# Five-tile second-layer loop begun tile by tile, and two row transposes issued by ScalarE

## The chip, the cores and the metric

One NeuronCore of one Trainium2 chip runs the whole program. The metric is device time in microseconds (us) of one execution; the time shown for a kernel is the median of its runs. PE is TensorE (PEld its weight loads), DVE is VectorE, ACT is ScalarE, POOL is GpSimd, SP is SyncE, whose queue (SPq) issues nearly all DMAs.

## The reference

Three stages follow each other. Causal attention with a cumulative bias (2 batches, 8 heads, 576 positions, 64 wide) gives a matrix x of 1152 tokens by 512. A dense layer follows, and then a routed layer with 8 experts:

```python
h = x @ w_in                      # 512 -> 2048
g = h * np.cos(h)
x = g @ w_out                     # 2048 -> 512

logits = x @ w_gate               # 8 experts
expert_idx = np.argmax(logits, axis=1)
...                               # softmax weight; each expert takes up to 288 tokens, in order
h = np.maximum(np.einsum('ecd,edf->ecf', disp, w1), 0.0)    # 512 -> 1024
y = np.einsum('ecf,efd->ecd', h, w2)                        # 1024 -> 512
out[i] = gate_w[i] * y[expert_idx[i], pos[i]]
```

## The kernel before, in words

Matrix products are made from pairs of float16 numbers (a high and a low part), three products each. After attention, `l1` (L509) makes g for 16 blocks f of 128 hidden columns and 3 chunks of 384 tokens: 48 groups of 12 matmuls, each in a PSUM bank that ACT and DVE read (L522, L523, L531) before it is free again. Six banks (tags s, pt and mm, two each) rotate; two more have the tags xv and sm.

The second matmul of the dense layer works on nine token tiles of 128 tokens, T0 to T8. `l2_mm` (L566) issues the three matmuls of one tile and one f into the tile's bank, 48 matmuls for a tile. `l2_wide` (L572) takes the first five tiles at once: T0 in bank xv, T1 in bank sm, T2 to T4 in the next banks of the rotation, which the last groups of `l1` have just used. Its loop goes over f outside and over the tiles inside, so that the sequence of PE is f = 0 of T0 to T4, then f = 1 of T0 to T4, and so on. At each f it first calls `feed` twice; that is the decoding of one more block of w_out (L456 to L458, then the split at L428 on ACT and L429 on DVE) and, when these are through, the loads (L672, L676) and splits of the first expert's eight weight pieces. `wout_dec` puts the decoding of block f behind the last eviction of block f + 8 of `l1`.

When a tile's 48 matmuls are done, `l2_end` (L555) writes its row buffer: ACT the high part (L561), DVE the low part (L562), POOL the token number (L563).

Then comes routing. `route_a` (L594) brings the row into transposed form: for T0 to T6 with one DMA transpose from the row buffer into a tile `xr` (two buffers) issued on SP's queue (L598), for T7 and T8 with PE transposes (L603, with ACT copies at L559 and L605). `route_b` (L608) makes the logits on PE (L620, 12 small matmuls), then a chain of small steps on DVE (L630 to L649), ACT (L631, L640) and PE (L637 to L639), and last an indirect DMA on POOL's queue (L650) that scatters the rows to their experts' places in a DRAM buffer `disp`.

`l2r` (L812) interleaves this with the second matmul of T5 to T8: T0 is transposed at step 0, T1 at step 2, and so on; a step is two f, or six matmuls, and routing's second half follows two steps later. T5 comes at step 10, T6 at step 16. After T4 and after T7, `partial` (L860) picks the expert that has the most tokens so far; SP reads its number into a register (L873), and only then can the weights of that expert be loaded. Before T7's second half, `hook` (L1013) gathers the first two experts' rows from `disp` by DMA transposes on SP's queue (L716, L723), which needs the scatters of T0 to T6 to have landed. Expert weights pass through three staging buffers `ws` of 512 KB; a load waits until ACT (L428) and DVE (L429) have split the piece that lay there.

The order in which each engine and each queue executes is fixed when the program is built. A planner goes through the program by its own estimate of when each instruction is ready, with program order as the priority, so a later instruction may be placed before an earlier one. At run time each engine and queue waits in that fixed order. The planner also adds all waits, on data and on buffers.

Of the kernel before, what the change touches and what calls it, by code (L numbers as in the profile page):

```python
# [11 lines left out]
F16 = mybir.dt.float16  # L12
# [11 lines left out]
WO0 = 8  # L24
W3P = 12
L2F = 2
NK = 3
NF = 1
NH = 2
PT = 5  # L30
WN = 5
# [40 lines left out]
def kernel(ctx, tc, q, k, v, s, w_in, w_out, wg, w1, w2, out, cap, wide):  # L72
    nc = tc.nc
    B, H, S, D = q.shape
    NP = H // 2
    DM, DFF = w_in.shape
    E, _, F = w1.shape
# [3 lines left out]
    KF = DFF // 128  # L81
# [10 lines left out]
    PTILE = PT - 1  # L92
    R0 = E - NK
    PROFILES = [[min(n, NS) for n in p] for p in SIZES]
    LIMITS = [[(n + 1) * E for n in p[NK:]] + [BIG * -1.0] * NH + [n + 1 for n in p[:NK]] for p in PROFILES]

# [22 lines left out]
    def bank(tag, bufs=2, dt=F32):  # L119
        return ps.tile([128, 512], dt, tag=tag, bufs=bufs, name=f"ps_{tag}")  # L120

    def any_bank():
        t, b = BANKS[rot[0] % 3]
        rot[0] += 1
        return bank(t, b)
# [429 lines left out]
    def l2_end(T, xp):  # L555
        r = work.tile([128, ROW], I32, tag="row", name="row", bufs=6)
        xf = xq[:, 0:DM] if T >= NDT else None
        if T >= NDT:
            nc.scalar.activation(xf, xp, AF.Copy, scale=2.0 ** -2)  # L559
        rh = r[:, 0:DM].bitcast(F16)  # L560
        nc.scalar.activation(rh[:, 0:DM], xp, AF.Copy, scale=2.0 ** -8)  # L561
        nc.vector.scalar_tensor_tensor(rh[:, DM:2 * DM], xp, 2.0 ** -8, rh[:, 0:DM], ALU.mult, ALU.subtract)  # L562
        nc.gpsimd.tensor_copy(r[:, DM + 1:ROW], tokid[:, T:T + 1])  # L563
        rows[T] = (r, xf)

    def l2_mm(xp, T, f):  # L566
        c, i = divmod(T, TPC)
        ts = slice(i * 128, (i + 1) * 128)
        for n, (a, w_) in enumerate(((0, 0), (0, 1), (1, 0))):
            gate["pe"] = nc.tensor.matmul(xp, lhsT=G[c][:, a, f, ts], rhs=wout[w_][:, f, :], start=(f == 0 and n == 0), stop=(f == KF - 1 and n == 2))  # L570

    def l2_wide(tiles, feed, per):  # L572
        xps = {T: bank(*WT[i]) if i < len(WT) else any_bank() for i, T in enumerate(tiles)}
        for f in range(KF):
            for _ in range(per):
                next(feed, None)
            for T in tiles:
                l2_mm(xps[T], T, f)
            yield
        for T in tiles:  # L580
            l2_end(T, xps[T])
        yield
# [11 lines left out]
    def route_a(T):  # L594
        r, xf = rows[T]
        if T < NDT:
            xr = work.tile([128, 2 * KD, 128], F16, tag="xr", name="xr", bufs=2)
            nc.sync.dma_start_transpose(out=xr, in_=r[:, 0:DM].bitcast(F16))  # L598
            rows[T] = (r, xr)
        else:  # L600
            tp = bank("pt")
            for kk in range(KD):
                nc.tensor.transpose(tp[:, kk * 128:(kk + 1) * 128], xf[:, kk * 128:(kk + 1) * 128], idf)  # L603
            xt = xq[:, DM:2 * DM].rearrange("p (k t) -> p k t", k=KD)
            nc.scalar.copy(xt.rearrange("p k t -> p (k t)"), tp)  # L605
            rows[T] = (r, xt)
# [55 lines left out]
    def e_weights(plan, lo=0, hi=None):  # L662
        n = KD + KE // 2
        items = [(e, src, i) for e, src in plan for i in range(n)][lo:hi]
        pend = []

        def ld(e, src, i):
            t = staging()
            src = src() if callable(src) else src
            if i < KD:  # L670
                s1 = w1[e, i * 128:(i + 1) * 128, :] if src is None else w1v[bass.ds(src * DM + i * 128, 128), :]
                nc.sync.dma_start(t, s1)  # L672
            else:
                j = (i - KD) * 256
                s2 = w2[e, j:j + 256, :] if src is None else w2v[bass.ds(src * F + j, 256), :]
                nc.sync.dma_start(t.rearrange("p (a d) -> p a d", a=2), s2.rearrange("(a p) d -> p a d", p=128))  # L676
            pend.append(t)

        todo = list(items)

        def fill(n):
            while todo and len(pend) < n and not (callable(todo[0][1]) and todo[0][1]() is None):
                ld(*todo.pop(0))

        fill(len(ws) - 1)
        yield
        for e, src, i in items:
            fill(len(ws))
            b_ = (win, wb[0:2], wb[2:4], wout)[e % 4]
            a = [b_[0].rearrange("p a b -> p (a b)").rearrange("p (k c f) -> p k c f", k=KD, c=2), b_[1].rearrange("p a b -> p (a b)").rearrange("p (k c f) -> p k c f", k=KE, c=2)]  # L690
            ew[e] = a
            t = pend.pop(0)
            if i < KD:
                after("ev cnt", split, a[0][:, i, 0, :], a[0][:, i, 1, :], t, 64.0)
            else:
                j = (i - KD) * 2
                after("ev cnt", split, a[1][:, j:j + 2, 0, :], a[1][:, j:j + 2, 1, :], t.rearrange("p (a d) -> p a d", a=2), 64.0)
            yield
# [93 lines left out]
    def run(*gens):  # L792
        live = [[g, n, 0.0] for g, n in gens]
        while live:
            live.sort(key=lambda z: z[2])
            z = live[0]
            try:
                next(z[0])
                z[2] += 1.0 / z[1]
            except StopIteration:  # L800
                live.remove(z)

    def take(gen, n):
        for _ in range(n):
            next(gen, None)
            yield

    def seq(*gens):
        for g in gens:
            yield from g  # L810

    def l2r(tiles, hook):  # L812
# [13 lines left out]
        for T in tiles:  # L826
            for j in range(KF // 2):
                next(gen)
                if mid and step - mid[0][1] >= RD:
                    finish()  # L830
                if pend and step % RP == 0:
                    mid.append((pend[0], step))
                    route_a(pend.pop(0))
                step += 1
                yield
            pend.append(T)
        for T in pend:
            while mid and len(mid) >= 1:
                finish()
            mid.append((T, step))  # L840
            route_a(T)
# [7 lines left out]
    def fixed():  # L849
        V = nc.vector  # L850
        pick = P["pick"] = work.tile([1, NK, E], F32, name="pick", bufs=1)
        keys = P["keys"] = work.tile([1, E], F32, name="keys", bufs=1)
# [27 lines left out]
    def counts():  # L880
# [8 lines left out]
        fl = work.tile([1, 1], I32, tag="fl", name="fl", bufs=1)  # L889
        pr = work.tile([1, NK + NH, E], F32, tag="pr", name="pr", bufs=1)  # L890
        ov = work.tile([1, len(LIMITS), E + NH], F32, tag="ov", name="ov", bufs=1)
# [4 lines left out]
        for i in range(NH):  # L896
            V.tensor_tensor(pr[:, i, :], pp[0:1, E:2 * E], pick[:, i, :], ALU.mult)
        for i in range(NK):
            V.tensor_tensor(pr[:, NH + i, :], pp[0:1, 0:E], pick[:, i, :], ALU.mult)
# [12 lines left out]
    def registers(fl, si):  # L912
        order = [nc.values_load(si[0:1, r:r + 1], engines=SP, min_val=0, max_val=E - 1) for r in range(E - NK)]
        first = [nc.values_load(si[0:1, E + h:E + h + 1], engines=SP, min_val=0, max_val=(E - 1) * NS + HEAD) for h in range(NH)]
        return order, first
# [84 lines left out]
    with ExitStack():  # L1000
        if True:
# [4 lines left out]
            items = KD + KE // 2  # L1006
            pre = e_weights([(i, i if i < NF else (lambda i=i: P["o"][i] if i < len(P["o"]) else None)) for i in range(NK)])
            run((l2_wide(range(WN), seq(wo, take(pre, items + 1)), L2F), KF + 1))
            xa = early.enter_context(tc.tile_pool(name="xa", bufs=1, side="right"))
            e_buffers(xa)  # L1010
# [78 lines left out]
```

## Time and profile before

| | us |
|---|---|
| median of 3 runs | 465.89 (465.44 to 466.89) |
| the profiled execution's own time | 467.52 |
| span of its instructions | 465.6 |
| PE busy | 422.9 (91%) |
| DVE busy | 329.9 (71%) |
| ACT busy | 290.3 (62%) |
| POOL busy | 122.3 (26%) |

The profile is of one execution. Times in the trace are us from the first instruction. A line of the timeline gives the start, the length, engine, source line, operation, the tiles written and read, the shape and how many neighbours are merged in it; in square brackets stands how long the engine was idle before it and what ended that. Matmuls are pipelined: a merged row of three lasts longer than the step from it to the next row. The chain of waits follows the work that ended last back from the end. `SPq` rows show when SP issues a DMA, not when it lands.

### The profile page before, as it was taken

How to read it: one execution, taken by the hardware profiler on the slowest of the kernel's cores; microseconds unless marked ns; L12 is line 12 of the kernel's file. 1: busy time of each engine (PE TensorE's matmuls, PEld its weight loads, DVE VectorE, ACT ScalarE, POOL GpSimd, SP SyncE). 2: the span in 40 equal slices, each digit the busy share in tenths (PEclk: the TensorE clock that was granted, in tenths of full speed). 3: DMA queues.
4: the chain of work that ended last, by engine and by line, in shares of the span. 5: the costliest groups of instructions: out<-in, count | busy, mean ns of one | idle time of the engine just before them, and what ended most of it. 6: DMA issues, size and time to landing. Idle time of an engine off the chain costs nothing.

```text
span 465.6 us, 10963 instructions
## 1 busy us (share of the span) xinstructions
PE 422.9 (91%) x4036; PEld 289.4 (62%) x4036; DVE 329.9 (71%) x847; ACT 290.3 (62%) x674; POOL 122.3 (26%) x205
## 2 busy tenths in 40 slices
PE   1879998889999999999899999979799999988994
PEld 1556665666756665555344445434698899888962
DVE  7757889787899955788888665475571477667670
ACT  3867888787777776777722453253663576677670
POOL 7231323240125544545430002201002110220231
PEclk9989999999999999999999999999999999998998
DMA  5899998998995410121245755794869978977851
GB/s 122 228 182 183 176 177 178 191 195 222 282 293 199 137 48 0 45 77 67 86 154 174 232 147 125 176 283 119 261 188 223 139 204 290 294 267 276 284 175 45
DMA packets 112653, 83.14 MB, mean 179 GB/s; under 512 B 85430, under 2 KB 93622, under 8 KB 112591
## 3 DMA queue, kind: packets, MB, share of 16 engines
q1 hardware_dynamic: 110335, 77.63, 63.7%
q0 software_dynamic: 2256, 4.73, 3.1%
q8 instruction: 33, 0.54, 0.5%
q14 instruction: 29, 0.24, 0.2%
HBM read 57.47 MB, written 12.14 MB: 150 GB/s over the span
## 4 chain that ended last, share of the span: by engine, by line
PE 51%; DVE 15%; DMA 15%; issue 6%; ACT 6%; SPq 4%; POOL 2%; POOLq 0%; DVEq 0%; ACTq 0%
DMA ws<-in_moe_w_dram 10%; PE ps_mm L375 5%; PE ps_mm L570 4%; PE ps_s L517 4%; PE ps_pt L347 4%; PE ps_pt L517 3%; PE ps_mm L517 3%; PE ps_s L769 3%; PE ps_s L305 3%; DVE y L523 2%; PE ps_mm L747 2%; PE ps_pt L747 2%; PE ps_s L570 2%; PE ps_xv L570 2%; PE ps_pt L570 2%
## 5 line engine op out<-in xcount | busy, mean ns | idle before, releaser
L517 PEld LDWEIGHTS <-win 128*128 128x128 f16 x576 | 56.0, 98 | 40.3 <-issue 4.6
L570 PEld LDWEIGHTS <-gall 128*128 128x128 f16 x432 | 40.8, 98 | 49.3 <-issue 2.5
L570 PE MATMUL ps_mm<-wout,gall 128*128 128x512 f16 x240 | 56.3, 379 | 1.6 <-DVE n__3030 L531 1.6
L429 DVE SCALAR_TENSOR_TENSOR gall<-ws,gall 128x1024 f16<-128x1024 f32 x32 | 38.6, 1221 | 23.4 <-ACT gall L428 23.1
L428 ACT ACTIVATE gall<-ws 128x1024 f16<-128x1024 f32 x32 | 33.6, 1057 | 25.9 <-DMA ws<-in_moe_w_dram 25.7
L756 POOL DMA_INDIRECT out_dram<-gall,eM x16 | 20.5, 1282 | 100.6 <-ACT gall L755 92.9
L428 ACT ACTIVATE wout<-ws 128x512 f16<-128x512 f32 (+1 forms) x32 | 27.2, 860 | 26.5 <-DVE ws L458 18.3
L429 DVE SCALAR_TENSOR_TENSOR win<-ws,win 128x512 f16<-128x512 f32 (+1 forms) x32 | 31.2, 981 | 11.1 <-ACT win L428 10.2
L429 DVE SCALAR_TENSOR_TENSOR wout<-ws,wout 128x512 f16<-128x512 f32 (+1 forms) x32 | 30.4, 957 | 11.0 <-ACT wout L428 10.2
L308 ACT ACTIVATE z<-z,st 128x128 f32<-128x128 f32 (+3 forms) x64 | 35.4, 556 | 4.0 <-DVE st L307 3.6
L650 POOL DMA_INDIRECT disp<-row,rsli x9 | 9.8, 1089 | 92.9 <-ACT rm L631 48.5
L305 PE MATMUL ps_s<-kT,qT 128*128 128x128 f16 (+3 forms) x128 | 25.7, 310 | 9.3 <-DVE st L307 6.5
L517 PE MATMUL ps_s<-xT,win 128*128 128x384 f16 x192 | 34.1, 326 | 0.0
L517 PE MATMUL ps_pt<-xT,win 128*128 128x384 f16 x192 | 33.9, 326 | 0.0
L517 PE MATMUL ps_mm<-xT,win 128*128 128x384 f16 x192 | 33.8, 326 | 0.0
L428 ACT ACTIVATE win<-ws 128x512 f16<-128x512 f32 (+1 forms) x32 | 27.4, 860 | 9.8 <-DMA ws<-in_moe_w_dram 9.7
L375 PE MATMUL ps_mm<-pp,vf 128*64 128x128 f32 x320 | 33.0, 285 | 0.0
L307 DVE CUSTOM_DVE_ANT_0 z<-ps_s,zm 128x128 f32<-128x128 f32 (+3 forms) x64 | 29.2, 482 | 4.0 <-PE ps_s L305 3.9
L347 PE MATMUL ps_pt<-idf,z 128*128 128x128 f32 x160 | 29.5, 287 | 0.8 <-DVE pp L349 0.6
L747 PEld LDWEIGHTS <-gall 128*128 128x128 f16 x480 | 28.1, 97 | 1.8 <-DVE gall L429 0.8
L530 ACT ACTIVATE y<-y,quarter 128x384 f32<-128x384 f32 x48 | 29.1, 605 | 0.0
L375 PEld LDWEIGHTS ps_mm<-pp,vf 128*64 128x64 f32 x320 | 20.9, 136 | 9.2 <-issue 7.1
(523 smaller groups left out, 926.5 us busy)
## 6 DMA issues: line engine op xcount, KB each, us to landing
ws<-in_moe_w_dram SPq DMA_DIRECT2D x64, 512.0 KB
ws<-in_moe_w_in_dram SPq DMA_DIRECT2D x16, 512.0 KB
ws<-in_moe_w_out_dram SPq DMA_DIRECT2D x16, 512.0 KB
disp<-zc SPq DMA_DIRECT2D x18, 257.0 KB
out_dram<-zc SPq DMA_DIRECT2D x9, 256.0 KB
qf<-in_q_dram SPq DMA_DIRECT2D x16, 128.0 KB
kf<-in_k_dram SPq DMA_DIRECT2D x16, 128.0 KB
vf<-in_v_dram SPq DMA_DIRECT2D x16, 128.0 KB
```

The costliest lines, as they stand in the source:

```text
L305: nc.tensor.matmul(sp[:, 0:w], lhsT=qT[:, c, h * FULL + t, :], rhs=kk, start=(c == 0), stop=(c == 1))
L307: gate["dve"] = nc.vector.tensor_tensor_reduce(z[:, 0:w], sp[:, 0:w], zm[:, W512 + 128 - w:W512 + 128], SC, 3e38, ALU.add, ALU.min, st[:, ...
L308: nc.scalar.activation(z[:, 0:w], z[:, 0:w], AF.Exp, bias=st[:, 0, h:h + 1], scale=-1.0, accum_out=sm_[:, 0, h:h + 1])
L347: nc.tensor.transpose(pt[:, j * 128:(j + 1) * 128], zs[h][:, j * 128:(j + 1) * 128], idf)
L375: nc.tensor.matmul(xv[h * 64:h * 64 + 64, ts], lhsT=vf[:, h * FULL + j, :], rhs=pv[h][:, j * 128:(j + 1) * 128], start=(j == 0), stop=(j = ...
L428: nc.scalar.activation(hi, src, AF.Copy, scale=sc)
L429: (eng or nc.vector).scalar_tensor_tensor(lo, src, sc, hi, ALU.mult, ALU.subtract)
L517: nc.tensor.matmul(hp[:, 0:CH], lhsT=win[a][:, kk, fs], rhs=xT[:, x_, kk, xs], start=(n == 0), stop=(n == 3 * KD - 1))
L530: nc.scalar.activation(y, y, AF.Sin, scale=TWO_PI, bias=quarter)
L570: gate["pe"] = nc.tensor.matmul(xp, lhsT=G[c][:, a, f, ts], rhs=wout[w_][:, f, :], start=(f == 0 and n == 0), stop=(f == KF - 1 and n == 2))
L747: gate["pe"] = nc.tensor.matmul(hp[:, 0:ns], lhsT=a1[:, kk, a, fs], rhs=X[:, x_ * KD + kk, 0:ns], start=(n == 0), stop=(n == 3 * KD - 1))
L756: sc = nc.gpsimd.indirect_dma_start(out=out, out_offset=bass.IndirectOffsetOnAxis(ap=M[:, b, 1:2].bitcast(U32), axis=0), in_=y, in_offset= ...
```

## The change

There are two edits. `l2_wide` first calls `feed` for three f, then issues f = 0, 1, 2 for T0, then f = 0, 1, 2 for T1, and so on to T4; from f = 3 on the loop is as before. The number of matmuls, their operands and the banks are unchanged. And the DMA transposes of T5 and T6 (`T >= WN`, with WN = 5) are issued by ACT on its own DMA queue; those of T0 to T4 stay on SP's.

```diff
+FH = 3
...
     def l2_wide(tiles, feed, per):
         xps = {T: bank(*WT[i]) if i < len(WT) else any_bank() for i, T in enumerate(tiles)}
-        for f in range(KF):
+        for f in range(FH):
+            for _ in range(per):
+                next(feed, None)
+        for T in tiles:
+            for f in range(FH):
+                l2_mm(xps[T], T, f)
+        for f in range(FH, KF):
             for _ in range(per):
                 next(feed, None)
             for T in tiles:
...
             xr = work.tile([128, 2 * KD, 128], F16, tag="xr", name="xr", bufs=2)
-            nc.sync.dma_start_transpose(out=xr, in_=r[:, 0:DM].bitcast(F16))
+            (nc.scalar if T >= WN else nc.sync).dma_start_transpose(out=xr, in_=r[:, 0:DM].bitcast(F16))
```

## Rows read from the trace of the kernel before

**Rows 1.** Page, parts 0 and 1: the span and the busiest engine.
```profile
span 465.6 us, 10963 instructions
PE 422.9 (91%) x4036; PEld 289.4 (62%) x4036; DVE 329.9 (71%) x847; ACT 290.3 (62%) x674; POOL 122.3 (26%) x205
```

**Rows 2.** Busy time by stretch: window, length, PE, PEld, DVE, ACT, POOL, PEclk, DMA.
```profile
276.50:300.00 23.50, 22.97 (x188) 11.40 (x186) 14.72 (x85) 6.69 (x23) 5.31 (x7) 1.00 0.62 132
300.00:320.00 20.00, 17.12 (x98) 8.22 (x95) 12.54 (x23) 10.84 (x15) 3.12 (x4) 1.00 0.81 240
```

**Rows 3.** Timeline where the five-tile loop begins, PE and DVE.
```profile
223.37 0.81 PE L570 MATMUL ps_xv<-wout,gall 128*128 128x512 f16 x3
...
225.00 0.56 DVE L531 SCALAR_TENSOR_TENSOR n__3009<-ps_pt,y 128x384 f32<-128x384 f32 x1
...
227.43 0.56 DVE L531 SCALAR_TENSOR_TENSOR n__3030<-ps_mm,y 128x384 f32<-128x384 f32 x1 [0.35 <-POOL gall L539]
...
228.04 0.81 PE L570 MATMUL ps_mm<-wout,gall 128*128 128x512 f16 x3 [1.63 <-DVE n__3030 L531]
...
228.69 0.81 PE L570 MATMUL ps_xv<-wout,gall 128*128 128x512 f16 x3
```

**Rows 4.** Timeline where the five-tile loop ends and routing begins.
```profile
274.59 1.22 DVE L429 SCALAR_TENSOR_TENSOR win<-ws,win 128x1024 f16<-128x1024 f32 x1 [0.82 <-ACT win L428]
...
275.74 0.68 DVE L562 SCALAR_TENSOR_TENSOR row<-ps_xv,row 128x512 f16<-128x512 f32 x1
...
276.45 15.31 SPq L598 DMA_TRANSPOSE xr<-row  x6
...
281.14 0.45 PE L620 MATMUL ps_s<-wgs,xr 128*128 128x8 f16 x12
```

**Rows 5.** DMA view of 270 to 316: busy tenths in 40 slices, and packets.
```profile
DMA  7910003990092294695997322999899898997828
...
DMA packets 9783, 8.13 MB, mean 177 GB/s; under 512 B 7632, under 2 KB 7632, under 8 KB 9779
```

**Rows 6.** Chain of waits, from T4's transpose on: start, us, what.
```profile
287.55 6.11 DMA xr<-row
...
298.42 5.57 DMA ws<-in_moe_w_dram
...
316.09 3.61 DMA disp<-row,rsli
...
326.38 6.89 DMA ws<-in_moe_w_dram
```

**Rows 7.** Timeline around T5's transpose: ACT and DVE steps of T5, T3 and T4.
```profile
289.58 0.69 DVE L562 SCALAR_TENSOR_TENSOR row<-ps_mm,row 128x512 f16<-128x512 f32 x1
...
290.73 0.20 ACT L631 ACTIVATE rm<-rm 128x1 f32<-128x1 f32 x1 [1.18 <-DVE rm L630]
...
291.22 0.19 ACT L640 ACTIVATION_READ_ACCUMULATOR rex<-ps_s,rm 128x1 f32 x1
...
294.20 0.17 DVE L630 TENSOR_REDUCE rm<-ps_s 128x1 f32<-128x8 f32 x1 [0.47 <-PE ps_sm L638]
```

**Rows 8.** SP's queue, narrow windows: T5's transpose as issued.
```profile
290.52 1.23 SPq L598 DMA_TRANSPOSE xr<-row  x1
```

**Rows 9.** Timeline around T6's transpose: DVE, ACT, SP's queue and PE.
```profile
303.94 0.68 DVE L562 SCALAR_TENSOR_TENSOR row<-ps_mm,row 128x512 f16<-128x512 f32 x1
304.01 1.06 ACT L428 ACTIVATE gall<-ws 128x1024 f16<-128x1024 f32 x1 [0.76 <-DMA ws<-in_moe_w_dram]
...
304.65 1.29 SPq L598 DMA_TRANSPOSE xr<-row  x1
...
306.35 7.79 SPq L676 DMA_DIRECT2D ws<-in_moe_w_dram  x4
...
309.77 0.46 PE L620 MATMUL ps_s<-wgs,xr 128*128 128x8 f16 x12 [2.76 <-DMA xr<-row]
```

**Rows 10.** Waits of SP's queue in 236 to 330: total, times, longest us.
```profile
SPq L716 <- DMA disp<-row,rsli: 5.6, 1, 5.6
```

## The prediction

> **What bounds the kernel now.** I read the profile's page first: PE is busy for 91% of the span [rows 1], so PE is the first suspect, and a wait of PE is worth what it lasts only where the next stage is waiting for PE. The table by stretch shows where PE is not full: 22.97 of 23.5 us while T0 to T4 are routed, then 17.12 of 20 us from 300 on, with the DMA engines at 0.81 [rows 2]. The granted clock is 1.00 in both, so no time is lost or won there. The chain of waits says what holds this part: T4's transpose takes 6.11 us, after it the register is read and the second expert's weights are loaded, then T6's scatter must land, and at 326.38 the third expert's weights begin to load [rows 6]. Everything after that hangs on that load, so what this change is worth is how much earlier it can start.
>
> In front of that chain stands one PE wait. The first matmul into T4's bank sat idle for 1.63 us, until the eviction that began at 227.43 and took 0.56 us freed the bank [rows 3].
>
> **Edit 1: three f for each tile first.** It removes no work and adds none: 240 matmuls (80 triples) before and after, only their order differs, and ACT, DVE and SP get the same instructions from `feed` in the same order, since the loop itself issues nothing but PE work. The six `feed` calls that now come ahead of the first matmul cost PE nothing, as PE waits only for decoded blocks f = 0, 1, 2; by its own ordering in the code block 2 was placed behind the eviction of block 10 of `l1`, which is long past.
>
> A triple takes 0.65 us (228.04 to 228.69 in rows 3). From 223.37 the new order runs T0 to 225.3, T1 to 227.3, T2 to 229.2, T3 to 231.2, and only then needs T4's bank, which is free at 228.0. T3's bank is free at 225.56 (225.00 plus 0.56) and is now wanted at 229.2; T2's, the one before it in the rotation, is freed earlier still [rows 3]. So the whole stall goes: **-1.63 us** for PE, and every bank has some 3 us to spare.
>
> What is late next? At the end of the loop T0's row cannot come earlier: the last weight split holds DVE from 274.59 to 275.81, and T0's low part starts then at 275.74, at once behind it; the transpose follows at 276.45 [rows 4]. But what the chain takes from T0 is its logits at 281.14, which stand in PE's queue behind the first 18 matmuls of T5, that is, at a place that PE reaches 1.63 us earlier, at 279.5. Is xr there by then? The slices of the DMA view are 1.15 us long. The transposes of T0 and T1 are the 3, 9, 9 from 276.9 to 280.35, with nothing after them [rows 5]; T0's is the first half, so it is there at about 279.2, 2.75 us after issue (an estimate from these slices). Bounds: it may be there at 279.2, so all of the 1.63 us passes, or only at 281.1, so nothing does. I take the first, nearest to the slices, less a rounding: **-1.6 us** at T0's logits. T2's transpose waits for them, T4's for T2's, so the shift is handed on to T4, to the register and to the loads.
>
> **Edit 2, T5.** SP is rid of 1.23 us at 290.52 [rows 8], but has nothing else to do then: the next thing in its queue is the register that T4 must deliver for the load at 298.42 [rows 6]. Gain 0. ACT gets an issue of presumably the same 1.23 us. ACT is busy for 6.69 us of 23.5 here [rows 2], so room there is; what counts is who queues behind it. T5's row is ready at 290.27 (289.58 plus 0.69), just ahead of T3's two ACT steps from 290.73 to 291.41 [rows 7]. If they are put off by the issue alone, T3 ends later by 0.8 us, and nobody waits for T3: T4's DVE steps begin at 294.20. Lower bound 0; upper bound 1.9 us, worked out as the first rival. I take 0, the row's own distance to T4 being 2.8 us.
>
> **Edit 2, T6.** SP is rid of 1.29 us at 304.65, yet the load behind it, at 306.35, waits for a staging buffer [rows 9], so again nothing is gained on SP. ACT gets 1.29 us next to the split at 304.01. If the issue stands ahead of that split, ACT waits for the row until 304.62, and the split starts at about 305.9 instead of 304.01, so the remaining loads of this expert slide by up to 1.9 us. Their cover is the 5.6 us that SP waits for T6's scatter after the last of these loads [rows 10]; without it they would cost their 1.9. What does count is when T6's xr lands: 304.65 to 309.77 is 5.1 us, against T0's 2.75, because loads are ahead of it in the same queue. On ACT's own queue it may land after 2.75 (-2.4 us), or, if the engines share their time evenly with the loads, after 1.2 of issue plus twice 2.75, or 6.7 (+1.6). T4's 6.11, shared with scatters from another queue [rows 6], is the nearest row and lies between T6's 5.1 and that end, so I take **0**.
>
> **Sum.** -1.6 + 0 + 0 = -1.6 us. The profiled execution took 467.52 us, 1.9 over its span; 467.52 - 1.6 is 465.9. It lies 1.63 above the median of the runs, so against the median 465.89 the forecast is **464.3 us**.
>
> **Rivals.**
>
> *ACT is held for T4's transpose.* If transposes of two queues may not be in flight together, T5's on ACT must wait until T4's, on SP, has landed at 293.66 (287.55 plus 6.11); before, both were in one queue and T5's was issued 3.1 us ahead of that landing [rows 6, 8]. The Trainium skill, "DMA: Bandwidth & Descriptors", section "Silent corruption: two transposing streams in flight at once", says that the later stream's first transpose has to wait for the earlier stream's full completion; no run yet shows the two side by side. What it costs depends on the planner's place for it. Ahead of T3's ACT steps, those end at 293.66 + 1.23 + 0.68 = 295.6; DVE's last steps for T3 wait for them, and T4's first step, at 294.20, is behind these in DVE's queue, so it starts at about 296.1, 1.9 us late [rows 7]. For: T5's row is ready before T3's steps. Against: the planner can see the wait and place the issue behind them, where it delays only T4's ACT steps: the issue ends at 294.9, half a us after T4's first DVE step (294.20 plus 0.17). Time: 465.89 - 1.6 + 1.9 = 466.2.
>
> *T6's transpose starves beside the loads (slower).* The DMA engines serve two queues by turns. T6's transpose is 1090 small packets (7632 by 7 tiles); the other 2151 packets of this stretch are at most 269 for each of the eight loads [rows 5]. If turns go packet by packet, a small one for a large one, 1090 need about four loads to pass, at some 2.5 us each (four issues in 7.79 us, rows 9): 9.7 us instead of 5.1, +4.6. It decides as soon as loads are in flight without a break from 304.65 on, and the slices of 8 and 9 there say that they are [rows 5]. The Trainium skill, "DMA: Bandwidth & Descriptors", section "SWDGE vs HWDGE vs iDMA", says that an engine goes round-robin over its internal queues; the rows do not show by what unit. Against: T4's transpose, beside scatters, was lengthened but not stopped. Time: 465.89 - 1.6 + 4.6 = 468.9.
>
> *The gain is not passed on.* T0's xr lands at 281.1 after all, so PE only waits elsewhere, and the edit does nothing: 465.9.
>
> **How the numbers follow.** A measurement of this kernel can tell about 0.3%, 1.4 us, from no change. Forecast 0.50, of which 0.08 ends within 0.3%, since -1.6 is near that bound; ACT held 0.17, 0.03 of it slower; starving 0.18, slower; not passed 0.15. So faster 0.42, same 0.08 + 0.14 + 0.15 = 0.37, slower 0.21. The range goes from -3.6 (the forecast with most of T6's possible 2.4) to +1.3 (ACT held, plus half a us for its delay of T4's steps and as much for T6's landing): 462.3 to 467.2. It leaves out the starving case and a little below. The forecast's own range is 462.3 to 465.4.
>
> **What would show it.** Right: no idle time at L570 before the first ps_mm triple; PE's last ps_pt triple of the loop, and T0's logits, 1.6 us earlier; the register and its first load near 296.8; T6's xr landing about 5 us after issue; the third expert's load near 324.8. The ACT rival shows as a gap on ACT ending with `DMA xr<-row`, with L631 of T3 or T4 behind it, and DVE's L630 of T4 late. The starving one shows as a longer wait of PE at L620 of T6 and a longer wait of SP at L716. I am wrong altogether if the loads of the third expert start earlier and the end does not, that is, if something after 330 takes the time back.

## The result, and the profile after

The changed kernel took **471.0 us** (median of 22 runs, 466.8 to 475.7). The kernel before, run in turn with it, took 467.7 (22 runs). The ratio is 1.0063, 95% interval 1.0040 to 1.0086: **slower, by 2.9 us**, where 1.6 us less was forecast. In a second comparison (f1 below) it was 1.0054 [1.0019, 1.0089]. The forecast stood on the 465.89 of three runs of the kernel before; 1.8 us of the distance between 464.3 and 471.0 is that base. Ratios, fits and counts of profiles leave out executions more than 1.5% above the fastest of their kernel (5 of the 22 of the changed kernel, 7 of the 12 of u3 below), and nothing here shows what lengthened those.

A first surprise is that the two profiled executions are alike in length. Page of the changed kernel, span and busiest engines:

```profile
span 465.7 us, 10964 instructions
PE 423.2 (91%) x4036; PEld 289.8 (62%) x4036; DVE 330.5 (71%) x847; ACT 291.1 (63%) x674; POOL 122.2 (26%) x205
```

Against [rows 1] that is the same span, 467.41 us of its own time against 467.52. One execution of each can't show 0.6%: the executions of the changed kernel that count differ by 7 us among themselves. So the profiles below are read for what happens in them, and the ratios say what it is worth.

In the code of after, line numbers are higher by one up to the loop and by seven behind it (L570 is L571, L598 is L605, L620 is L627, L639 is L646).

**The start of the loop.** Timeline of PE (start, length, then as in the rows of before):

```profile
223.10 2.10 PE L571 MATMUL ps_xv<-wout,gall 128*128 128x512 f16 x9
225.04 2.11 PE L571 MATMUL ps_sm<-wout,gall 128*128 128x512 f16 x9
226.99 2.10 PE L571 MATMUL ps_s<-wout,gall 128*128 128x512 f16 x9
```

Nine matmuls for each tile, no idle time: the 1.63 us of [rows 3] are gone, as forecast. **Where the loop ends**, PE's timeline shows what became of them:

```profile
280.23 0.46 PE L627 MATMUL ps_s<-wgs,xr 128*128 128x8 f16 x12 [1.28 <-DMA xr<-row]
```

The transpose was issued at 276.97, behind the last weight split on DVE. PE now arrives early and waits 1.28 us for it; in [rows 4] it came late enough not to wait.

**T5.** Timeline of ACT and its queue, of DVE, and of PE, around T5's transpose, answering to [rows 7]:

```profile
291.78 1.36 ACTq L605 DMA_TRANSPOSE xr<-row  x1
293.18 0.20 ACT L638 ACTIVATE rm<-rm 128x1 f32<-128x1 f32 x1 [4.53 <-PE ps_sm L645]
...
293.81 0.15 DVE L653 TENSOR_SCALAR rm<-rm 128x1 f32<-128x1 f32 x1 [2.63 <-ACT rex L647]
...
294.27 0.15 DVE L637 TENSOR_REDUCE rm<-ps_s 128x1 f32<-128x8 f32 x1
...
295.20 0.17 PE L646 MATMUL ps_sm<-roh,tri 128*128 128x16 f16 x1 [1.49 <-DVE roh L641]
```

T5's row was complete at 289.38 (its low part began at 288.69 and took 0.69), but the issue came only at 291.78. PE read T4's transposed row from 292.12 on, so it came as that row had landed. T3's two ACT steps (L638, L647) stand behind it. T3's last DVE steps wait for those (2.63 us, L653), and T4's first DVE step L637 at 294.27 is behind them: 2.15 us behind T4's logits at 292.12, where it was 0.49 before (294.20 against 293.71). That is the first rival.

**T6.** Timeline of ACT's queue, PE and DVE, answering to [rows 9]:

```profile
305.35 1.25 ACTq L605 DMA_TRANSPOSE xr<-row  x1
...
310.14 0.49 PE L627 MATMUL ps_s<-wgs,xr 128*128 128x8 f16 x12 [4.16 <-DMA xr<-row]
310.48 4.43 PE L571 MATMUL ps_mm<-wout,gall 128*128 128x512 f16 x10
314.70 0.22 PE L646 MATMUL ps_sm<-roh,tri 128*128 128x16 f16 x1
...
314.98 0.17 DVE L648 TENSOR_SCALAR rt<-ps_sm 128x8 f32<-128x8 f32 x1 [2.14 <-PE ps_sm L646]
...
315.26 1.22 DVE L430 SCALAR_TENSOR_TENSOR gall<-ws,gall 128x1024 f16<-128x1024 f32 x1
```

The row lands 4.8 us after issue (305.35 to 310.14), so the transpose itself costs what was forecast. But PE waits 4.16 us for it in place of 2.76: between T5's last small matmul and T6's logits the planner has put 35 matmuls of T6 and T7 where there were 40, presumably since it expects a transpose on a free queue to land sooner. And then ten matmuls take 4.43 us, almost twice their time. The table by stretch says why (window, length, busy time of PE, PEld, DVE, ACT, POOL, granted clock, DMA share, GB/s):

```profile
276.50:300.00 23.50, 20.73 (x177) 10.29 (x176) 15.21 (x86) 6.26 (x23) 5.27 (x7) 1.00 0.54 128
300.00:320.00 20.00, 15.84 (x77) 6.89 (x76) 10.59 (x22) 9.47 (x13) 2.80 (x4) 0.83 0.79 242
306.00:308.50 2.50, 0.00 (x0) 0.00 (x0) 1.16 (x2) 1.06 (x1) 0.00 (x0) 1.00 0.90 239
308.50:315.30 6.80, 5.16 (x25) 2.14 (x26) 2.95 (x14) 3.67 (x6) 0.00 (x0) 0.50 0.82 250
```

From 300 to 320 the granted clock is 0.83 where [rows 2] have 1.00. PE is idle from 306.0 on; from 308.5 to 315.3 the clock stands at 0.50, its lower level of 1.2 GHz, and then at 1.00 again. The Trainium skill, "TensorE: Matmul & The Clock Gate", Part 1, says that a monitor sets the clock by how busy PE has lately been; the rows agree as far as the order goes, idle first, low clock behind it.

T6's L646 at 314.70 (311.91 before) holds DVE for 2.14 us, with the split L430 behind it, so the staging buffers come free late. SP's queue, first of the changed kernel, then (the last row) of the kernel before:

```profile
316.51 0.37 SPq L683 DMA_DIRECT2D ws<-in_moe_w_dram  x1
321.01 1.35 SPq L723 DMA_TRANSPOSE eX<-disp  x1
...
327.41 1.59 SPq L679 DMA_DIRECT2D ws<-in_moe_w_dram  x3
...
325.12 1.59 SPq L672 DMA_DIRECT2D ws<-in_moe_w_dram  x3
```

The second expert's last weight load is issued at 316.51 (before: 313.76), the third expert's first one at 327.41 (before: 325.12), 2.3 us late, though everything up to T4's logits was early.

What holds that load is no longer what [rows 6] show. There the chain of waits runs from T6's scatter at 316.09 through SP's gathers to the load. In the changed kernel it runs through PE (start, us, what):

```profile
305.35 4.74 DMA xr<-row
...
310.62 4.29 PE ps_mm L571 x10
314.92 5.03 PE ps_mm L571 x22
...
322.98 0.79 PE ps_s L624 x8
...
326.38 0.15 DVE keys L885
...
328.06 5.67 DMA ws<-in_moe_w_dram
```

T6's landing, the ten matmuls at 0.50 and the matmuls behind them delay T7's logits (L624), and the register that the load needs comes from these. SP still waits for T6's scatter, 4.1 us in place of 5.6, and then 1.5 us more for the register. The chain takes this way through PE in all six counted profiles that have T6 on ACT and its logits where the planner puts them; with T6 on SP it goes by the scatter in six of nine.

### The profile page after: what moved, and what is told of

Its sections match the earlier page's. It is cut to its first block, busy times and chain, and to the rows that moved or that the text cites. A ratio compares the mean times of both kernels' runs of the same rounds, so it can differ in the third digit from the quotient of the medians.

```text
span 465.7 us, 10964 instructions
## 1 busy us (share of the span) xinstructions
PE 423.2 (91%) x4036; PEld 289.8 (62%) x4036; DVE 330.5 (71%) x847; ACT 291.1 (63%) x674; POOL 122.2 (26%) x205
## 4 chain that ended last, share of the span: by engine, by line
PE 43%; DVE 19%; DMA 19%; ACT 6%; issue 5%; SPq 4%; POOL 3%; ACTq 0%; DVEq 0%; POOLq 0%
DMA ws<-in_moe_w_dram 10%; PE ps_mm L571 5%; PE ps_s L518 4%; PE ps_mm L376 4%; PE ps_pt L518 3%; PE ps_mm L518 3%; PE ps_s L776 3%; PE ps_pt L348 3%; DVE ws L458 2%; DMA qT<-qs 2%; PE ps_pt L754 2%; PE ps_mm L754 2%; PE ps_s L306 2%; PE ps_pt L776 2%; SPq L232 2%
## 5 line engine op out<-in xcount | busy, mean ns | idle before, releaser
L571 PEld LDWEIGHTS <-gall 128*128 128x128 f16 x432 | 41.4, 99 | 50.4 <-issue 4.7
L571 PE MATMUL ps_mm<-wout,gall 128*128 128x512 f16 x240 | 58.4, 390 | 0.0
L430 DVE SCALAR_TENSOR_TENSOR gall<-ws,gall 128x1024 f16<-128x1024 f32 x32 | 38.7, 1220 | 20.6 <-ACT gall L429 20.5
L763 POOL DMA_INDIRECT out_dram<-gall,eM x16 | 20.7, 1291 | 97.9 <-ACT gall L762 90.2
L430 DVE SCALAR_TENSOR_TENSOR win<-ws,win 128x512 f16<-128x512 f32 (+1 forms) x32 | 31.4, 982 | 11.6 <-ACT win L429 11.2
L430 DVE SCALAR_TENSOR_TENSOR wout<-ws,wout 128x512 f16<-128x512 f32 (+1 forms) x32 | 30.3, 956 | 9.2 <-ACT wout L429 9.2
```

The costliest lines, as they stand in the source:

```text
L430: (eng or nc.vector).scalar_tensor_tensor(lo, src, sc, hi, ALU.mult, ALU.subtract)
```

## The experiments

All keep the line numbers of before. Each was timed side by side with the kernel before on one chip, in four sets of four kernels and a last one of two.

### First set: the parts one by one

**e1** is the first edit alone, **e2** the second alone; **e3** moves only T6's transpose, **e4** only T5's, both with the old loop.

```diff
-        for f in range(KF):                                     # e1
+        [next(feed, None) for f in range(FH) for _ in range(per)], [l2_mm(xps[T], T, f) for T in tiles for f in range(FH)]
+        for f in range(FH, KF):
...
-            nc.sync.dma_start_transpose(...)
+            (nc.scalar if T >= WN else nc.sync).dma_start_transpose(...)    # e2; e3: T == 6; e4: T == 5
```

> Edit 1 alone: three f for each tile first, all transposes on SP. It leaves the order on ACT, DVE, SP and POOL as before. Forecast of the prediction: the stall of 1.63 us goes and the end comes 1.6 us earlier (ratio 0.9965). Theory now: T0's row waits for the last weight split on DVE, whose load is paced by the three staging buffers and not by PE, so T0's logits come only some 0.9 us earlier, and the register for the second expert's loads too: ratio 0.997 to 1.000. If the loss of the whole change lay in this edit, the ratio would be 1.006.

> Edit 2 alone: T5's and T6's transposes issued by ACT, loop as before. If edit 2 carries the loss and edit 1 hides a part of it, the ratio is 1.007 to 1.010, the first load of the third expert at about 328 instead of 325. If edit 1 carries the loss, the ratio is 1.000.

> Only T6's transpose on ACT, T5's stays on SP, loop as before. Theory A (T6's issue stands on ACT between two weight splits, these and the loads behind them slide, and T7's second half and the third expert's register come late): ratio 1.005 to 1.009, the last load of the second expert issued 2 to 3 us later than 313.8. Theory B (T5's wait for T4's landing is the loss): ratio 0.999 to 1.002.

> Only T5's transpose on ACT, loop as before. It stands on ACT ahead of T3's L631. Theory B (ACT is held until T4's transpose has landed, DVE and PE behind it): T4's first DVE step 1 to 2 us later than 294.2, the register and the second expert's first load as much later than 298.4, ratio 1.003 to 1.006. Theory A: the delay is there in the trace, but has little weight at the end, ratio 0.999 to 1.003.

Measured: e1 0.9957 [0.9928, 0.9986], e2 1.0047 [1.0010, 1.0084], e3 0.9993 [0.9968, 1.0019], e4 1.0006 [0.9973, 1.0039]. In this set the loss comes with the second edit, and the first one gains by itself, below its theory's 0.997 to 1.000 and near the prediction's 0.9965; two repeats below don't hold that gain. e2 lies between its two theories. Neither half of the second edit shows a loss alone, though both traces show the delay that was named for it. In e4's profile T4's L630 is 2.27 us behind its logits, in e3's it is 0.49: what happens at T5 is T5's doing. At T6, e3 with the old loop and T5 on SP shows all that the change shows, the second expert's last load included (316.28). Its timeline of PE, and the stretch from 300 to 320:

```profile
309.90 0.48 PE L620 MATMUL ps_s<-wgs,xr 128*128 128x8 f16 x12 [3.94 <-ACT gall L428]
310.24 4.43 PE L570 MATMUL ps_mm<-wout,gall 128*128 128x512 f16 x10
314.46 0.22 PE L639 MATMUL ps_sm<-roh,tri 128*128 128x16 f16 x1
...
300.00:320.00 20.00, 16.06 (x76) 6.83 (x75) 10.54 (x22) 9.51 (x14) 3.08 (x4) 0.83 0.79 240
```

### Second set: the parts on the new loop

**f1** is the change again, **f2** the new loop with T6 moved, **f3** the new loop with T5 moved. **f4** is the whole change, but with T5's issue bound behind T3's last ACT step:

```diff
+            with tc.issue_after(gate['ex3'].ins) if T == 5 else ExitStack():     # ex3: T3's L640
                 (nc.scalar if T >= WN else nc.sync).dma_start_transpose(...)
```

> The change as it is, once more, beside its parts on one chip. If the parts add up (loop 0.9957, T5 1.0006, T6 0.9993), the ratio is 0.996; the first timing of the change gave 1.0063. Theory: the two transposes on ACT do harm that the loop's gain does not outweigh, ratio 1.003 to 1.007.

> Edit 1 with only T6's transpose on ACT. The first expert loads as early as with edit 1 alone (1.2 us earlier than before). Theory A (T6's issue on ACT lets T7's second half and the third expert's register come late): third expert's first load near 327 instead of 324.6, ratio 1.000 to 1.004. Theory B (T5's wait is the loss): ratio 0.995 to 0.998, as edit 1 alone.

> Edit 1 with only T5's transpose on ACT. Theory B: ACT is held for T4's landing, T4's first DVE step starts 1.8 us late, the gain of edit 1 for the register is used up, ratio 1.000 to 1.004. Theory A: ratio 0.995 to 0.999.

> The whole change, but T5's issue on ACT is placed behind T3's last ACT step instead of ahead of it; nothing else differs in ACT's order. If the place is what costs, T4's first DVE step starts again within 0.6 us of T4's logits, the second expert's first load about 1 us earlier than in the change as it is, and the ratio falls by 0.002 to 0.004 against that. If T5's late landing itself costs, nothing is gained.

Measured: f1 1.0054 [1.0019, 1.0089], f2 1.0065 [1.0024, 1.0106], f3 1.0040 [1.0000, 1.0080], f4 0.9996 [0.9961, 1.0030]. With either half on the new loop the kernel is some 2 to 3 us behind the kernel before, and no more with both; f3's interval just reaches 1, and f2 lies above both its ranges. f4 isn't told from the kernel before. Its timeline of ACT and DVE shows what the placing does:

```profile
292.19 0.20 ACT L631 ACTIVATE rm<-rm 128x1 f32<-128x1 f32 x1 [1.18 <-DVE rm L630]
...
294.10 1.77 ACTq L598 DMA_TRANSPOSE xr<-row  x1
...
294.96 0.17 DVE L630 TENSOR_REDUCE rm<-ps_s 128x1 f32<-128x8 f32 x1 [1.03 <-PE ps_sm L638]
```

T3's step goes first, the issue still waits for T4's landing, and T4's L630 is 0.49 us behind the logits (294.47) again. But PE then waits 5.64 us at T6's logits, with the clock at 0.83 from 300 to 320, so T6's part is still there. That leaves f4 in part unexplained: it has T6's part like f2, one transpose more on ACT, and a lower ratio than f2 (1.0065) and its repeat r4 (1.0044).

### Third set: does T6 cost by its place, T5 by its place alone?

**r1** is e1 again. **r2** is the new loop with T5's placed issue and T6 on SP. **r4** is f2 again, and **r3** is f2 with T6's second half told two steps later, which puts 43 matmuls ahead of its logits in place of 35 (counted as above):

```diff
-                if mid and step - mid[0][1] >= RD:
+                if mid and step - mid[0][1] >= RD + 2 * (mid[0][0] == 6):    # r3
```

> The first edit alone, a second time, beside the three others of this call. Theory (the loop's gain of about 2 us is real and both moved transposes lose it again): ratio 0.994 to 0.998 against before, no idle time in front of the first ps_mm triple of L570, and the fastest of the four kernels of this call. Rival (the 0.9957 of the first time was chance, and the loop is worth nothing): ratio 0.998 to 1.002, no faster than the kernel with T5 placed.

> The first edit, and T5's transpose on ScalarE placed behind T3's last step on ScalarE; T6 stays on SyncE. Theory (T5 costs only by where its issue stands): like the first edit alone within 0.3%, T4's DVE step L630 0.5 us behind T4's logits, ratio 0.994 to 0.999. Rival (a transpose on a second queue costs by itself, as a wait of transposes of one queue for those of the other): T6's transpose on SyncE has to wait for T5's on ScalarE or the issue on ScalarE holds the splits; the second expert's last load 1.5 us or more later, ratio 1.001 to 1.005.

> The first edit, T6's transpose on ScalarE, and T6's second half (logits and what follows) told two steps later, so that in the order of TensorE the logits stand behind more of T7's matmuls and, in the order of VectorE, a weight split stands ahead of T6's steps. Theory (T6 costs by the early place that the planner gives its logits): TensorE's wait at T6's logits is under 2 us in place of about 4, the second expert's last weight load lies 1.5 to 2.5 us earlier than in the kernel without the delay, and the ratio to before falls from about 1.006 to 0.997 to 1.002. Rival (T6 costs by its transpose, which runs beside the loads on another queue): the loads and the end stay as late as in the kernel without the delay, ratio 1.004 or more.

> The first edit and T6's transpose on ScalarE, a second time, as the partner of the kernel with T6's second half told later. Theory (T6's move alone loses what the loop gains): ratio 1.003 to 1.008, TensorE waits 3.9 us or more at T6's logits, VectorE waits for T6's L639 with a split behind it, third expert's first load 104 us or more behind the loop's start where it is 101 with the first edit alone. Rival (T6 alone costs nothing, as in the run with the old loop): ratio within 0.3% of that of the first edit alone.

Measured: r1 0.9988 [0.9958, 1.0018], r2 1.0016 [0.9986, 1.0046], r3 1.0045 [1.0009, 1.0080], r4 1.0044 [1.0011, 1.0078]. r1's ratio lies in its rival's range, its interval reaches into its theory's, and it is the fastest of the four, as the theory wanted; so it decides little. r2's ratio lies in the rival's range, but its interval reaches into the theory's, and the rival's sign is missing: the second expert's last load is issued 91.0 us behind the loop's start, against 90.2 in e1, where the rival wanted 1.5 more. T4's step is 0.48 us behind the logits. So the trace shows nothing of T5's delay any more, and the time decides nothing. r4 repeats f2.

r3 did in the trace what the theory said, and not in the time, where its 1.0045 is in the rival's range. Timeline of PE and the stretch from 300 to 320:

```profile
309.82 0.46 PE L620 MATMUL ps_s<-wgs,xr 128*128 128x8 f16 x12 [1.55 <-DMA xr<-row]
...
300.00:320.00 20.00, 17.28 (x96) 7.98 (x93) 12.37 (x23) 10.73 (x15) 4.18 (x4) 1.00 0.81 247
```

PE waits 1.55 us, the clock stays at 1.00, and the second expert's last load is issued 89.8 us behind the loop's start where r4 has 94.5. The chain goes by T6's scatter again. That profiled execution took 467.5 us, one of the kernel's quickest; its median was 470.8. This sent me to the clock of every execution. Over 311 executions (the fit further down) the span rises by **3.4 us (+-0.4) for each 0.01 that the mean granted clock is lower**, a link between the two and not yet a cause. And the mean clock differs between kernels: 0.983 for f1 and 0.982 for f2, 0.987 for the kernel before on the same chip.

### Fourth and fifth set: PE kept busy while it waits

If a wait of PE costs twice, once by its length and again by the clock behind it, work that fills the wait must help, though it is useless work. **u1** has five more matmuls ahead of T0's logits (their result is overwritten by the logits); every other engine has the order of e1. **u2** has eight more ahead of T6's, **u3** is the whole change with five and twelve (in both, T6's second half is told one step later). **u4** is the kernel before.

```diff
+        fill = lambda: [nc.tensor.matmul(lb, lhsT=G[2][:, 0, KF - 1, 256:384], rhs=wout[0][:, KF - 1, :],
+                        start=True, stop=True) for _ in range({0: 5}.get(T, 0))]
-        after("pe", logits)
+        after("pe", fill), after("pe", logits)
```

> The first edit alone with five more matmuls (128x512, written into the bank that T0's logits overwrite next) ahead of T0's logits on TensorE; every other engine has the order of the first edit alone. Clock theory (TensorE's idle time at T0's logits, which the first edit makes, lets the clock fall behind it in some executions): no stretch of granted clock 0.50 between 277 and 300, mean clock over the runs 0.986 or more where the first edit alone had 0.9859 and 0.9843, ratio 0.993 to 0.998. Rival (the falls there are chance or have another cause): mean clock as before, ratio 0.996 to 1.001.

> As the last, and eight such matmuls ahead of T6's logits, whose second half is told one step later so that the planner doesn't put the added matmuls in the place of T7's. Clock theory: no stretch of 0.50 from 305 to 320 either, mean clock 0.988 or more, ratio 0.991 to 0.996, so faster than both kernels. Rival (a fall there delays nothing that the end waits for): mean clock higher, but the ratio no better than that of the kernel with T0 filled alone.

> The whole change, with five such matmuls ahead of T0's logits and twelve ahead of T6's, told one step later. Clock theory: the 6.8 us at 0.50 behind the wait for T6 are gone, ten matmuls of T7 behind the logits take 2.2 us where they took 4.43, mean clock 0.986 or more where the change had 0.981 and 0.982, ratio 0.998 to 1.002. Order theory (T5's held issue and T6's early steps delay the chain whatever the clock): ratio 1.003 or more, though the clock is up.

> The kernel before, unchanged, beside itself. Ratio 0.997 to 1.003 by every theory. Clock theory: TensorE waits about 2.8 us at T6's logits and nowhere at T0's, so no stretch of 0.50 between 277 and 300, and one of 3.4 us behind T6's wait in some executions; mean clock 0.986 to 0.988.

Measured: u1 0.9985 [0.9945, 1.0025] with a mean clock of 0.988 where before had 0.987; u2 1.0000 [0.9958, 1.0043] at 0.990; u3 1.0029 [0.9982, 1.0076] at 0.989, on five executions only; u4 0.9982 [0.9941, 1.0023]. The clock does what the theory says in all three, the time hardly: none of them is told from before by these intervals. u1 lies in the rival's range, and the unchanged kernel u4 came out as low. u2 missed its 0.991 to 0.996. u3 lies between its two theories: T5's held issue is still in it (T4's L630 2.55 us behind the logits), and its other engines' order changed too, so it settles nothing about T6.

Without e1 beside it u1 couldn't be judged, so e1 (**v1**) and u1 (**v2**) ran side by side:

> The first edit alone, a third time. Theory (the loop brings T0's logits 0.7 to 0.9 us earlier where the stall was 1.63, and the idle time that it leaves in front of them lets the clock fall in some executions): ratio 0.995 to 1.000, TensorE idle 1.1 us or more at T0's logits. Rival (the whole stall is gained, the second run was chance): ratio 0.993 to 0.997.

> The first edit with the five added matmuls ahead of T0's logits, beside the first edit alone on one chip. Clock theory: no stretch of 0.50 between 277 and 300, mean clock over the runs 0.002 or more above that of the first edit alone, and a ratio 0.002 to 0.004 lower. Rival (falls behind T0's wait are rare or cost nothing at the end): mean clock and ratio within 0.001 and 0.002 of the first edit alone.

Measured: v1 1.0006 [0.9970, 1.0042], mean clock 0.986; v2 0.9980 [0.9951, 1.0010], mean clock 0.989. That is the clock theory's difference, 0.0035 of clock and 0.0026 of time, though the two intervals overlap and v1 lies above both its ranges. The profiles show the place. First v1, timeline of PE at T0's and T1's logits, then the stretch behind them:

```profile
282.47 0.46 PE L620 MATMUL ps_s<-wgs,xr 128*128 128x8 f16 x12 [1.75 <-DMA xr<-row]
...
282.83 1.90 PE L570 MATMUL ps_mm<-wout,gall 128*128 128x512 f16 x5
...
284.60 2.69 PE L570 MATMUL ps_mm<-wout,gall 128*128 128x512 f16 x7
287.12 0.45 PE L620 MATMUL ps_s<-wgs,xr 128*128 128x8 f16 x12
...
282.00:288.00 6.00, 5.53 (x44) 2.62 (x45) 2.34 (x14) 2.04 (x5) 1.05 (x1) 0.72 0.41 80
```

And u1, the same views:

```profile
280.30 1.24 PE L612 MATMUL ps_s<-wout,gall 128*128 128x512 f16 x5
282.49 0.46 PE L620 MATMUL ps_s<-wgs,xr 128*128 128x8 f16 x12 [0.96 <-DMA xr<-row]
...
282.86 1.24 PE L570 MATMUL ps_mm<-wout,gall 128*128 128x512 f16 x5
...
283.96 1.67 PE L570 MATMUL ps_mm<-wout,gall 128*128 128x512 f16 x7
285.47 0.45 PE L620 MATMUL ps_s<-wgs,xr 128*128 128x8 f16 x12
...
282.00:288.00 6.00, 5.51 (x52) 2.91 (x53) 3.85 (x24) 2.40 (x7) 1.19 (x1) 1.00 0.58 112
```

T0's logits begin at 282.47 and 282.49, each 3.3 us behind the issue. Behind 1.75 us of idle time the clock falls to 0.72 of the stretch, the twelve matmuls take 4.6 us in place of 2.9, and T1's logits are 1.65 us later (287.12 against 285.47); the chain hands that on to T4 and to the second expert's loads. With the wait filled nothing falls there, in u1 as in v2.

At T6 the kernel before waits too, and in u4, as in the first profile of before, the clock holds behind that wait. u4's timeline of PE and stretch:

```profile
311.19 0.46 PE L620 MATMUL ps_s<-wgs,xr 128*128 128x8 f16 x12 [2.48 <-ACT gall L428]
311.51 1.89 PE L570 MATMUL ps_mm<-wout,gall 128*128 128x512 f16 x8
...
300.00:320.00 20.00, 17.38 (x96) 7.96 (x94) 11.98 (x29) 10.63 (x15) 3.30 (x4) 1.00 0.83 250
```

### All profiles together

| profiles | PE's wait at T0's logits, us | clock fell behind it | wait at T6's logits, us | clock fell behind it |
|---|---|---|---|---|
| old loop, T6 on SP (before, u4, e4) | 0 to 0.6 | 0 of 3 | 2.5 to 3.4 | 1 of 3 |
| new loop, T6 on SP (e1, v1, f3, r2) | 1.1 to 1.75 | 1 of 4 | 2.3 to 3.3 | 3 of 4 |
| the same, T0 filled (u1, v2) | 0.3 to 1.0, behind the fill | 0 of 2 | 2.5 to 2.7 | 1 of 2 |
| old loop, T6 on ACT (e2, e3) | 0 to 0.4 | 0 of 2 | 3.9 to 4.4 | 2 of 2 |
| new loop, T6 on ACT (after, f1, f4, r4) | 1.1 to 2.0 | 1 of 4 | 4.1 to 5.6 | 4 of 4 |
| T6's logits told later (r3, u2) | 1.3 and filled | 0 of 2 | 1.6 to 1.7 | 0 of 2 |

The clock falls in other places too. Each counted profile has it at 0.50 for some 3 to 7 us of the first 100 us, ahead of the loop, where the built programs have one order on every engine. In the first set the loops of e1, e3 and e4 begin at 223.1 to 223.5, and that of e2, with one such fall more, at 224.88. Windows of e3, then of e2:

```profile
0.00:100.00 100.00, 81.51 (x805) 56.91 (x806) 77.06 (x272) 73.49 (x208) 36.26 (x120) 0.98 0.90 182
0.00:100.00 100.00, 80.35 (x767) 55.41 (x769) 74.00 (x271) 73.06 (x207) 35.73 (x119) 0.97 0.90 178
```

So the mean clock of one execution says little of the change, and it takes many.

A least-squares fit over the 311 executions of before and of all these kernels but r3, u2 and u3 (the five sets, each its own level, one term for each part, 95% bounds) gives what each part is worth:

| part | span, us | mean clock | span at equal clock, us |
|---|---|---|---|
| new loop | +0.2 +-0.6 | -0.0024 +-0.0012 | -0.6 +-0.4 |
| T5 on ACT where the planner puts it | +1.1 +-0.7 | -0.0008 +-0.0014 | +0.8 +-0.5 |
| T6 on ACT | +1.2 +-0.6 | -0.0019 +-0.0013 | +0.6 +-0.4 |
| fill ahead of T0's logits | -1.0 +-1.0 | +0.0035 +-0.0021 | +0.2 +-0.7 |

A fifth term, for T5 on ACT and placed, is -0.6 +-0.9. The first three add up to +2.5 us, against the measured 2.5 and 2.9. Their clock terms add up to -0.0051, which at 3.4 us for 0.01 is 1.7 us; the rest, 0.8, is the last column's sum. So about two thirds of the loss come with the lower clock, though the fit can't say where in the execution it fell, and T5's clock term alone is not told from 0. That it is PE's idle time that brings the clock down is shown at T0 by filling it (the fill's clock term excludes zero, its time term only just); at T6 it rests on the profiles, since r3 and u2 removed the fall there and didn't gain the time.

## Why the prediction was wrong

Three terms of the sum failed. The two of edit 2, put at 0, cost time in the fit above: T5 +1.1 us, T6 +1.2. And the -1.6 of edit 1 came to 0.8 at T0's logits, with nothing to be told at the end (+0.2 +-0.6).

**What bounds the kernel.** The chain was read rightly for the kernel before, T4 to the loads and T6's scatter to the third expert. That another one, through T7's matmuls on PE, lay close behind was not seen, and with T6 on ACT that one decides. The failed sentence is "The granted clock is 1.00 in both, so no time is lost or won there". It was true of the profile of before and was taken for a property of the stretch: in e4, with the old loop and T6 on SP, the clock fell there. Nothing in the rivals made use of a clock that can change: this way to lose had no chance of its own. "Everything after that hangs on that load" went too far as well. With T6 on ACT (six counted profiles) the third expert's first load is issued 104.8 us behind the loop's start on average, with T6 on SP (nine) 102.6; from there to the end it is 138.2 and 139.4. So of some 2 us about 1.2 seem to come back by the end; where, no run shows.

**Edit 1, -1.63 us at PE: right.** There is no idle time at the start of the loop in any profile with the new loop.

**Edit 1, T0's logits, -1.6: the mis-sized term.** It rested on T0's row landing 2.75 us after its issue. With PE waiting for it, landing can be read off the logits: 3.26 to 3.36 us in all kernels with the new loop. From the loop's start, T0's logits come at 57.8 to 58.5 us in the five profiles with the old loop (mean 58.1), at 56.9 to 57.8 in the nine with the new loop and no fill (mean 57.3): **0.8 us earlier, not 1.6**. The other 0.8 and more became idle time at T0's logits, between the forecast and the rival "the gain is not passed on". The longer landing explains some 0.5 of it. The rest is the row: its transpose was issued 53.1 us behind the loop's start in the one profile that the forecast read, the earliest of all; the other counted profiles have 53.6 to 55.2, and in three of the five with the old loop PE waited for it already. The idle time at T0's logits had a price that the rival didn't name, the fall of the clock behind it. Three runs of the edit alone gave 0.9957, 0.9988 and 1.0006, on average -0.8 us, but two of them aren't told from no change.

**Edit 2, T5, taken as 0: wrong, the first rival happened.** Its bound of 1.9 us is close: T4's first DVE step moved from 0.49 to 2.15 us behind the logits, 1.7 us. PE's wait of 1.49 us at T4's L646 follows from it. "The planner can see the wait and place the issue behind them" was the wrong side: it put the issue ahead of T3's steps. The order of the built program (a listing of f1, which is the change with before's line numbers) has the held instruction and its waits:

```
L598 DMA_TRANSPOSE xr<-row 128x8x128 [waits DMAHW5,DMAHW4,DMAHW6,DMAHW3,DMAHW7,DVE,PE]
```

The five DMAHW are the completions of the five transposes of SP. That agrees with the rule of the Trainium skill cited in the prediction ("DMA: Bandwidth & Descriptors", "Silent corruption: two transposing streams in flight at once"). f4 and r2 show the cure in the trace, 0.48 to 0.49 us again.

**Edit 2, T6, taken as 0: the transpose was judged rightly, its followers not.** It lands after 4.8 us in the change, 4.6 to 6.4 in the other kernels that issue it on ACT, 4.5 to 5.3 from SP: neither the gain of 2.4 nor the starving of 4.6 came. What was missed is that moving the DMA moves the logits forward in PE's fixed order. PE waits 4.16 us for 2.76, the clock falls in every such profile, T6's L639 comes 2.8 us later, DVE stands behind it, and the splits and the last loads slide by 2.75. The cover named for the loads, SP's wait for T6's scatter [rows 10], held for them, and the scatter's own 1.5 us (317.57 for 316.09) don't hold the third expert either. T7's matmuls do, behind PE's wait and the low clock. r3 gives this part its test: with the later place of the logits the wait is 1.55 us and the load comes 102.1 us behind the loop's start, where r4 has 105.2.

**What would show it.** The signs set down for the first rival all appeared: ACT's gap, L631 of T3 behind the transpose, T4's L630 late. Of the starving rival's two signs PE's longer wait at T6's logits appeared, but from the earlier place of the logits: the transpose took 4.8 us, and SP's wait at L716 became shorter. "The loads of the third expert start earlier and the end does not" was not needed: they start later.

**What stays open.** How much of T6's cost is the order and how much the clock. Why f4 came out ahead of f2. Why r3, whose profile has T6 repaired, is as slow on average as r4: its mean clock is low (0.983), so the clock may fall elsewhere in its executions or not as in the profile; one profile of a kernel can't say. And whether any part of the change is worth keeping: the new loop with the filled wait came out at 0.9985 and 0.9980, ahead of the change (1.0063), but not told from the kernel before, whose own repeat u4 came out at 0.9982. No version here is shown to beat both.

## What to carry to other kernels

Before counting a removed PE stall as a gain, find the next operand that PE will wait for and read its landing from issue to use, in more than one profile: what it can't pass on turns into idle time there, and the clock may charge for it a second time. A DMA transpose that is moved to a second engine waits there for the first queue's transposes, so look at what stands behind it in that engine's order. And where a planner fixes the order by estimates, moving one DMA moves other work: compare the orders of all engines, and take the granted clock of several executions, not of one.

## What the runs showed of the hardware

- The granted clock isn't fixed for a kernel: executions of the change had means from 0.975 to 0.987. In the stretches read here it stood at 1.00 or 0.50, and fell during or behind waits of PE: in the change 0.50 from 308.5 to 315.3 after PE had been idle since 306.0, and ten matmuls took 4.43 us there, where eight take 1.89 at 1.00 (u4).
- A wait doesn't bring a fall each time: with T6's transpose on SP and waits of 2.3 to 3.4 us at its logits, the clock fell in five of nine profiles. So one profile doesn't show what the next execution will do.
- Two queues gave the transposes no earlier landing: T6's took 4.8 us from ACT's queue and 5.1 from SP's [rows 9], both beside the expert's loads. The issue took 1.25 to 1.77 us on ACT, 1.23 to 1.33 on SP.
